# Attention on one NeuronCore: the 64-row first query block and key chunk handled as 128 rows

## The chip, the cores and the metric

The kernel runs on one core of a Trainium2 chip. The metric is the device time of one execution in microseconds (us), the median over several runs. The engines of the core are PE (TensorE, with its weight loads listed apart as PEld), DVE (VectorE), ACT (ScalarE), POOL (GpSimd) and SP (SyncE, which issues the DMAs here).

## The reference

Inputs are `q`, `k`, `v` of shape 4 x 8 x 576 x 64 and a gate `f` of shape 4 x 8 x 576. For each batch entry and head:

```python
cum = cumsum(log(clip(f, 1e-4, 1)))
scores = q @ k.T / 8 + (cum[i] - cum[j])      # -1e9 where j > i
attn = softmax(scores)                         # with 1e-9 added to the sum
x = attn @ v
```

The heads are put side by side (2304 rows of 512) and go through two dense layers: first `max(x@w1, x@w2, x@w3) @ w_out` with 768 hidden columns, then `g(x @ w_in) @ w_out` with 2048 hidden columns, where `g` is a quotient of polynomials.

## The kernel before

The sequence of 576 rows is cut into five query blocks that are also the five key chunks: rows 0 to 64 and then four times 128 rows (`Q0`, `Q1`, L20 and L21). Blocks 0, 1, 2 form group 0 (320 queries), blocks 3 and 4 form group 1 (256 queries). Two heads of a batch entry form a `Pair`; a `Unit` is one head of a pair in one group. Batch entry 0 is done as four pairs with group 0 alone and then four pairs with group 1 alone; the other three entries as twelve pairs with both groups. That makes 20 pairs and 64 units, 32 of each group.

What a pair does ahead of its units (`prepare`, L301): `load` and `load_v` bring natural rows of q, k and v into tiles `qn`, `kn`, `v` of 128 partitions x 5 chunks x 2 heads x 64, by `load_nat` (L221). Block 0 has one DMA of its own, 64 partitions, both heads (L223); the others share a DMA for each head. `transposed` (L283) turns the blocks on PE into one PSUM tile `tk` or `tq`, one transposition for each block (L288). For block 0 it takes 64 rows of the tile and a 64 x 64 corner of the identity. A pair turns its keys of group 0 even if it has queries of group 1 alone, so there are 36 transpositions of a 64-row block: 20 of k and 16 of q. ACT, DVE and POOL then make the operands of the score product from the PSUM tile.

What a unit does, in three steps of the main loop (L537): in its first step `scores` (L321) multiplies query block `i` by all keys up to its end. The first six pairs use one product in full float32 (L340), the others two products in the split format (L342, L343). The query block is the stationary operand, 64 columns wide for block 0, the keys are streamed. DVE masks the scores, negates them and takes the row minimum (L344), ACT takes the exponential with the row sum (L350). `normalise` (L352) makes reciprocals on DVE and scales `e` on POOL (L360). `begin` sets, for group 0, the 64 unused rows of the row sums to one with a small POOL memset (L319). In the next step `turn` (L362) transposes the blocks of `e` on PE into a PSUM tile `tp`, key chunk by key chunk (L381), and ACT copies a bank of them to `pt` (L385). Key chunk 0 gives 64 partitions there, and block 0, which has chunk 0 alone, is transposed from 64 rows. `pt` is allocated for each pair and group under a tag with one buffer (L367). In the step after that `attend` (L387) multiplies, for both heads, `v` of each key chunk (stationary, 64 columns, head 0 to PSUM partitions 0 to 63, head 1 to the others) by the transposed probabilities, in float32 (L399). For key chunk 0 both operands have 64 partitions. There are 32 calls of `attend` that do work.

Around this, `fill` (L502) inserts work of other stages a fixed number of times in each step: conversions of weights for the first dense layer and later for the second (L151 to L170: DMA, ACT, DVE, POOL), and products of the first dense layer (L429 to L431, L453 to L455). After the last unit the rest of the first layer and the conversion of `w_in` follow, then the second layer (L669 to L720), to the end. In the first four pairs every fresh PSUM tile is first written by two products of a constant tile (`exercised`, L77). The instructions of each engine are put in order by the tile framework, which schedules with its own simulated timeline (`schedule_with_timeline_sim=True`), but for some DMAs that are kept in program order and the second layer, whose order is written out. In most of the calls of `attend` the scheduler runs the two passes of head 0 on key chunk 0 ahead, by themselves, and the rest later in one run.

Of the kernel before, what the change touches and what calls it, by code (L numbers as in the profile page):

```python
# [18 lines left out]

Q0 = [0, 64, 192, 320, 448]  # L20
Q1 = [64, 192, 320, 448, 576]  # L21
GQ = [(0, 320), (320, 576)]
GBLK = [(0, 1, 2), (3, 4)]

# [10 lines left out]
def kernel(  # L35
# [100 lines left out]
    for qf in qfs:  # L136
        nc.vector.tensor_copy(qf[D : D + 2], ones[0:2, :NA])


    w1t, wot = {}, {}  # L140

# [78 lines left out]

    def load_nat(dst, src, b, h0, i0, i1):  # L221
        if i0 == 0:
            nc.sync.dma_start(dst[0:D, 0], src[b, h0 : h0 + 2, 0:D].rearrange("h p d -> p h d"))  # L223
            i0 = 1
        for h in range(2):
            nc.sync.dma_start(
                dst[:, i0:i1, h], src[b, h0 + h, Q0[i0] : Q1[i1 - 1]].rearrange("(c p) d -> p c d", p=P)
            )
# [3 lines left out]
    class Pair:  # L232
# [50 lines left out]
        def transposed(self, nat, g, which):  # L283
            lo, hi = GQ[g]
            t = exercised(ps_t.tile([P, 512], F32, name=f"t{which}_{self.n}_{g}", tag="t"), self.n)
            for i in GBLK[g]:
                nr = Q1[i] - Q0[i]
                nc.tensor.transpose(  # L288
                    t[:, Q0[i] - lo : Q1[i] - lo],
                    nat[0:nr, i].rearrange("p h d -> p (h d)"),  # L290
                    ident[0:nr, 0:nr],
                )
            return t[:, : hi - lo]

        def copies(self):
# [12 lines left out]
    class Unit:  # L308
# [6 lines left out]
        def begin(self):  # L315
            self.st = apool.tile([P, 9], F32, name=f"st_{self.nm}", tag="st", bufs=3)
            self.rs = apool.tile([P, 2, 3], F32, name=f"rs_{self.nm}", tag="rs", bufs=3)
            if self.g == 0:
                nc.gpsimd.memset(self.rs[D:P, 0, 0:1], 1.0)  # L319

        def scores(self, i):  # L321
            p, h, g = self.pair, self.h, self.g
            if not p.whole:
                (k1, k2), (q1, q2) = k_split(p.ik[h]), q_split(g, p.iq[g][h])
            nr = Q1[i] - Q0[i]
            qs = slice(Q0[i] - GQ[g][0], Q1[i] - GQ[g][0])
            keys = Q1[i]
            self.e[i] = apool.tile([P, keys], F32, name=f"e{i}_{self.nm}", tag=f"e{i}_{h}")
            e = self.e[i]
            st = self.st  # L330
            n0 = 3 * (i - GBLK[self.g][0])
            nm = st[:nr, n0 : n0 + 2]
            l = self.rs[:nr, 0, i - GBLK[self.g][0] : i - GBLK[self.g][0] + 1]
            parts = [(0, keys)] if keys <= 512 else [(0, 320), (320, keys)]
            off = S - keys if nr == P else S - P - Q0[i]
            for n, (a, z) in enumerate(parts):
                sp = exercised(ps_s.tile([P, 512], F32, name=f"s{i}_{n}_{self.nm}", tag="s"), p.n)
                if p.whole:
                    kf, qf = kfs[p.ik[h]][: D + 2], qfs[p.iqf[h]][: D + 2]
                    nc.tensor.matmul(sp[:nr, : z - a], qf[:, qs], kf[:, a:z], start=True, stop=True)  # L340
                else:
                    nc.tensor.matmul(sp[:nr, : z - a], q1[:, qs], k1[:, a:z], start=True, stop=False)  # L342
                    nc.tensor.matmul(sp[:nr, : z - a], q2[:, qs], k2[:, a:z], start=False, stop=True)  # L343
                nc.vector.tensor_tensor_reduce(  # L344
                    out=e[:nr, a:z], in0=sp[:nr, : z - a], in1=mask[:nr, off + a : off + z],
                    scale=-1.0, scalar=3.0e38 if n == 0 else nm[:, 0:1],
                    op0=ALU.add, op1=ALU.min, accum_out=nm[:, n : n + 1],
                )
            m = nm[:, len(parts) - 1 : len(parts)]
            nc.scalar.activation(e[:nr], e[:nr], AF.Exp, bias=m, scale=-1.0, accum_out=l)  # L350

        def normalise(self):  # L352
            blks = GBLK[self.g]
            n = len(blks)
            nc.vector.tensor_scalar_add(self.rs[:, 0, :n], self.rs[:, 0, :n], 1.0e-9)
            nc.vector.reciprocal(self.rs[:, 1, :n], self.rs[:, 0, :n])  # L356
            for j, i in enumerate(blks):
                nr = Q1[i] - Q0[i]
                e = self.e[i]
                nc.gpsimd.tensor_scalar(e[:nr], e[:nr], self.rs[:nr, 1, j : j + 1], 0.0, op0=ALU.mult, op1=ALU.add)  # L360

        def turn(self, bank):  # L362

            g, p = self.g, self.pair
            hi = GQ[g][1]
            if g not in p.pt:
                p.pt[g] = apool.tile([P, 2, GCOLS[g]], F32, name=f"pt_{self.nm}", tag=f"pt{g}")  # L367
            pt = p.pt[g][:, self.h]
            chunks = GBANK[g][bank]
            tp = exercised(ps_t.tile([P, 512], F32, name=f"tp{bank}_{self.nm}", tag="t"), self.pair.n)  # L370
            base = GCH[g][chunks[0]][0]
            n = 0
            for c in chunks:
                col, q0 = GCH[g][c]
                kr = Q1[c] - Q0[c]
                for i in GBLK[g]:
                    if i < c:
                        continue
                    nr = Q1[i] - Q0[i]
                    dst = col - base + Q0[i] - q0  # L380
                    nc.tensor.transpose(  # L381
                        tp[:kr, dst : dst + nr], self.e[i][:nr, Q0[c] : Q1[c]], ident[:nr, :nr]
                    )
                n += hi - q0
            nc.scalar.activation(pt[:kr, base : base + n], tp[:kr, :n], AF.Copy)  # L385

        def attend(self):  # L387

            p, h, g = self.pair, self.h, self.g
            if h == 0:  # L390
                return
            lo, hi = GQ[g]
            w = hi - lo
            ot = exercised(ps_o.tile([P, 512], F32, name=f"o_{self.nm}", tag="o"), p.n)
            order = list(GCH[g].items())
            for j, (c, (col, q0)) in enumerate(order):
                kr = Q1[c] - Q0[c]
                for i in range(2):
                    nc.tensor.matmul(  # L399
                        ot[SIDES[i][0], q0 - lo : w], p.v[:kr, c, i], p.pt[g][:kr, i, col : col + hi - q0],  # L400
                        start=(j == 0), stop=(j == len(order) - 1),
                    )
            x = mpool.tile([P, 2, w], F32R, name=f"x_{self.nm}", tag=f"x{g}", bufs=(6, 8)[g])
            nc.scalar.activation(x[:, 0], ot[:, :w], AF.Copy)
            nc.vector.tensor_tensor(x[:, 1], ot[:, :w], r32(x[:, 0]), op=ALU.subtract)
            xt[p.b, p.hp, g] = x
# [389 lines left out]
```

## Time and profile before

| | us |
|---|---|
| median of 3 runs | 1014.16 (1014.15 to 1014.49) |
| the profiled execution | 1014.65 |
| its span, from the first instruction to the last | 1012.8 |
| PE busy | 984.6 (97%) |
| DVE busy | 750.6 (74%) |
| ACT busy | 613.5 (61%) |
| POOL busy | 286.7 (28%) |

Busy time of PE is counted with the modelled ends of the products, which overlap: one that starts 0.11 us after another is shown with 0.27 us. What a product costs in a run of products is the distance from its start to the next start. Attention with the first dense layer in its gaps takes the first 520 us or so, the rest of the first layer with the conversion of `w_in` until about 607 us, the second layer the rest.

### The profile page before, as it was taken

What the parts mean: (1) busy time and instruction counts of PE and PEld (TensorE: products, weight loads), DVE (VectorE), ACT (ScalarE), POOL (GpSimd) and SP (SyncE); (2) the same over time, 40 slices, a digit from 0 to 9 for tenths busy, and PEclk for the clock granted to TensorE, in tenths of its full rate; (3) what the DMA queues carried; (4) which work ended last, traced back from release to release, by engine and by line L of the source; (5) the groups of instructions that cost most, each with busy time, mean ns of one, the idle gap of its engine ahead of it and who ended that gap; (6) DMA issues with size and microseconds to landing.
All of it is one profiled execution on the core that took longest, in us unless ns stands there. A gap on an engine that the chain in (4) does not pass through costs nothing.

```text
span 1012.8 us, 16900 instructions
## 1 busy us (share of the span) xinstructions
PE 984.6 (97%) x5780; PEld 831.2 (82%) x5780; DVE 750.6 (74%) x1744; ACT 613.5 (61%) x1409; POOL 286.7 (28%) x498
## 2 busy tenths in 40 slices
PE   8989999999999999999998989999999999999998
PEld 5657778887888888988898987888888888899997
DVE  4779984555677676644349676988988888899997
ACT  4775665656655566554434336766766666677775
POOL 1545763543554554443326440000000000000000
PEclk9998999999999999999999999999999999999999
DMA  4574223213444355221034529301001100200000
GB/s 122 162 213 132 79 57 89 47 41 104 119 128 151 104 154 179 81 59 48 1 116 146 177 80 344 128 1 49 35 1 63 42 1 1 95 10 1 32 1 32
DMA packets 118453, 86.69 MB, mean 86 GB/s; under 512 B 67280, under 2 KB 103136, under 8 KB 118368
## 3 DMA queue, kind: packets, MB, share of 16 engines
q1 hardware_dynamic: 118368, 85.62, 27.9%
q8 instruction: 46, 0.75, 0.3%
q14 instruction: 39, 0.32, 0.1%
HBM read 62.90 MB, written 22.69 MB: 85 GB/s over the span
## 4 chain that ended last, share of the span: by engine, by line
PE 77%; DVE 14%; issue 3%; DMA 3%; ACT 2%; POOL 1%; SPq 0%; DVEq 0%; POOLq 0%; ACTq 0%
PE oo L719 7%; PE oo L720 7%; PE oo L718 6%; PE o L399 6%; PE hq L669 6%; PE hq L671 6%; PE hq L670 6%; PE tp L381 5%; PE h L429 5%; PE h L430 4%; PE h L431 4%; PE s L342 2%; PE x2p L453 2%; PE x2p L455 2%; PE x2p L454 2%
## 5 line engine op out<-in xcount | busy, mean ns | idle before, releaser
L429 PE MATMUL h<-x,w1h 128*128 128x320 f32 (+1 forms) x576 | 176.9, 307 | 2.1 <-DVE m L436 2.0
L430 PE MATMUL h<-x,w1h 128*128 128x320 f32 (+1 forms) x576 | 173.0, 300 | 0.0
L431 PE MATMUL h<-x,w1l 128*128 128x320 f32 (+1 forms) x576 | 172.7, 300 | 0.0
L360 POOL TENSOR_SCALAR e<-e,rs 64x64 f32<-64x64 f32 (+4 forms) x160 | 88.6, 565 | 114.5 <-DVE rs L356 87.9
L350 ACT ACTIVATE e<-e,st 64x64 f32<-64x64 f32 (+4 forms) x160 | 89.3, 558 | 51.7 <-DVE st L344 48.9
L429 PEld LDWEIGHTS h<-x,w1h 128*128 128x128 f32 x576 | 110.3, 192 | 8.8 <-DVE m L436 3.7
L719 PE MATMUL oo<-wp,gh 128*128 128x512 f32 x288 | 112.8, 392 | 0.0
L718 PE MATMUL oo<-wp,gh 128*128 128x512 f32 x288 | 112.4, 390 | 0.0
L430 PEld LDWEIGHTS h<-x,w1h 128*128 128x128 f32 x576 | 110.2, 191 | 2.2 <-issue 2.0
L344 DVE CUSTOM_DVE_ANT_0 e<-s,mask 128x320 f32<-128x320 f32 (+3 forms) x160 | 68.1, 432 | 57.6 <-PE s L343 37.3
L431 PEld LDWEIGHTS h<-x,w1l 128*128 128x128 f32 x576 | 110.0, 191 | 0.1
L720 PE MATMUL oo<-wp,gl 128*128 128x512 f32 x288 | 108.8, 392 | 0.0
L678 ACT ACTIVATE s<-hq 128x512 f32<-128x512 f32 (+1 forms) x80 | 44.3, 554 | 97.2 <-PE hq L671 97.1
L385 ACT ACTIVATE pt<-tp 128x384 f32<-128x384 f32 (+3 forms) x160 | 69.8, 471 | 31.6 <-PE tp L381 28.7
L399 PE MATMUL o<-pt,v 128*64 128x256 f32 (+3 forms) x512 | 83.0, 371 | 0.3 <-ACT pt L385 0.3
L381 PE MATMUL tp<-ident,e 128*128 128x128 f32 (+2 forms) x480 | 81.4, 278 | 0.6 <-POOL e L360 0.5
L681 DVE SCALAR_TENSOR_TENSOR s<-s,ab,u 128x512 f32<-128x512 f32 (+1 forms) x80 | 55.8, 698 | 31.8 <-ACT u L679 31.6
L671 PE MATMUL hq<-x,wil 128*128 128x512 f32 (+1 forms) x192 | 70.4, 366 | 0.0
L669 PE MATMUL hq<-x,wih 128*128 128x512 f32 (+1 forms) x192 | 70.4, 366 | 0.0
L670 PE MATMUL hq<-x,wih 128*128 128x512 f32 (+1 forms) x192 | 70.3, 366 | 0.0
L453 PE MATMUL x2p<-hh,wo 128*128 128x320 f32 (+1 forms) x192 | 59.6, 314 | 7.2 <-POOL hh L440 5.9
L381 PEld LDWEIGHTS tp<-ident,e 128*128 128x128 f32 (+2 forms) x480 | 54.3, 132 | 13.6 <-issue 7.0
(128 smaller groups left out, 2444.6 us busy)
## 6 DMA issues: line engine op xcount, KB each, us to landing
raw_w<-in_moe_w_dram SPq DMA_DIRECT2D x18, 512.0 KB
raw_wp<-in_moe_w_out_dram SPq DMA_DIRECT2D x32, 256.0 KB
wpd<-wp SPq DMA_DIRECT2D x32, 256.0 KB
raw_wi<-in_moe_w_in_dram SPq DMA_DIRECT2D x32, 256.0 KB
wp<-wpd SPq DMA_DIRECT2D x10, 768.0 KB
x2d<-xo SPq DMA_DIRECT2D x16, 320.0 KB
out_dram<-ob SPq DMA_DIRECT2D x18, 256.0 KB
kn<-in_k_dram SPq DMA_DIRECT2D x32, 128.0 KB
```

The source lines that it names most:

```text
L350: nc.scalar.activation(e[:nr], e[:nr], AF.Exp, bias=m, scale=-1.0, accum_out=l)
L381: nc.tensor.transpose(tp[:kr, dst : dst + nr], self.e[i][:nr, Q0[c] : Q1[c]], ident[:nr, :nr])
L399: nc.tensor.matmul(ot[SIDES[i][0], q0 - lo : w], p.v[:kr, c, i], p.pt[g][:kr, i, col : col + hi - q0], start=(j == 0), stop=(j == len(orde ...
L429: nc.tensor.matmul(hp_[:, :w], wh[:, j, dc], xs[dc][:, 1], start=(dc == NDC - 1), stop=False)
L430: nc.tensor.matmul(hp_[:, :w], wh[:, j, dc], xs[dc][:, 0], start=False, stop=False)
L431: nc.tensor.matmul(hp_[:, :w], wl[:, j, dc], xs[dc][:, 0], start=False, stop=(dc == 0))
L669: nc.tensor.matmul(hp_[:, :w], wih[:, dc, fs], xh, start=(dc == 0), stop=False)
L670: nc.tensor.matmul(hp_[:, :w], wih[:, dc, fs], xl, start=False, stop=False)
L671: nc.tensor.matmul(hp_[:, :w], wil[:, dc, fs], xh, start=False, stop=(dc == NDC - 1))
L718: nc.tensor.matmul(o, g[0][:, ts_], wh_, start=(fc == 0), stop=False)
L719: nc.tensor.matmul(o, g[0][:, ts_], wl_, start=False, stop=False)
L720: nc.tensor.matmul(o, g[1][:, ts_], wh_, start=False, stop=(fc == NF2 - 1))
```

## The change

Block 0 and key chunk 0 are given 128 rows. The loads of block 0 bring rows 0 to 127 of q, k and v. The transpositions of block 0 take 128 rows and the whole identity, and write 128 columns, of which the upper 64 are then overwritten by block 1. The scores of block 0 are computed for 128 queries against 64 keys. The attention product on chunk 0 reads 128 rows of `v` and of `pt`. Since the transposition of chunk 0 still gives only 64 rows, two lasting tiles `pts` take the place of the tile for each pair, and the lower half (partitions 64 to 127) of the columns of chunk 0 is set to zero once at the start. The memset of the unused row sums goes.

```diff
+    pts = []
+    for g in range(2):
+        pts.append(apool.tile([P, 2, GCOLS[g]], F32, name=f"pt{g}", tag=f"pt{g}"))
+        col = GCH[g][0][0]
+        nc.gpsimd.memset(pts[g][D:P, :, col : col + GQ[g][1] - GQ[g][0]], 0.0)
...
     def load_nat(dst, src, b, h0, i0, i1):
         if i0 == 0:
-            nc.sync.dma_start(dst[0:D, 0], src[b, h0 : h0 + 2, 0:D].rearrange("h p d -> p h d"))
+            nc.sync.dma_start(dst[:, 0], src[b, h0 : h0 + 2, 0:P].rearrange("h p d -> p h d"))
             i0 = 1
...
             for i in GBLK[g]:
-                nr = Q1[i] - Q0[i]
-                nc.tensor.transpose(
-                    t[:, Q0[i] - lo : Q1[i] - lo],
-                    nat[0:nr, i].rearrange("p h d -> p (h d)"),
-                    ident[0:nr, 0:nr],
-                )
+                at = Q0[i] - lo
+                nc.tensor.transpose(t[:, at : at + P], nat[:, i].rearrange("p h d -> p (h d)"), ident)
             return t[:, : hi - lo]
...
-            if self.g == 0:
-                nc.gpsimd.memset(self.rs[D:P, 0, 0:1], 1.0)
...
-            nr = Q1[i] - Q0[i]
-            qs = slice(Q0[i] - GQ[g][0], Q1[i] - GQ[g][0])
+            nr = P
+            qs = slice(Q0[i] - GQ[g][0], Q0[i] - GQ[g][0] + P)
...
-            off = S - keys if nr == P else S - P - Q0[i]
+            off = S - P - Q0[i]
...
-                nr = Q1[i] - Q0[i]
                 e = self.e[i]
-                nc.gpsimd.tensor_scalar(e[:nr], e[:nr], self.rs[:nr, 1, j : j + 1], 0.0, op0=ALU.mult, op1=ALU.add)
+                nc.gpsimd.tensor_scalar(e, e, self.rs[:, 1, j : j + 1], 0.0, op0=ALU.mult, op1=ALU.add)
...
             if g not in p.pt:
-                p.pt[g] = apool.tile([P, 2, GCOLS[g]], F32, name=f"pt_{self.nm}", tag=f"pt{g}")
+                p.pt[g] = pts[g]
...
-                    nr = Q1[i] - Q0[i]
                     dst = col - base + Q0[i] - q0
-                    nc.tensor.transpose(
-                        tp[:kr, dst : dst + nr], self.e[i][:nr, Q0[c] : Q1[c]], ident[:nr, :nr]
-                    )
+                    nc.tensor.transpose(tp[:kr, dst : dst + P], self.e[i][:, Q0[c] : Q1[c]], ident)
...
             for j, (c, (col, q0)) in enumerate(order):
-                kr = Q1[c] - Q0[c]
                 for i in range(2):
                     nc.tensor.matmul(
-                        ot[SIDES[i][0], q0 - lo : w], p.v[:kr, c, i], p.pt[g][:kr, i, col : col + hi - q0],
+                        ot[SIDES[i][0], q0 - lo : w], p.v[:, c, i], p.pt[g][:, i, col : col + hi - q0],
                         start=(j == 0), stop=(j == len(order) - 1),
                     )
```

## Rows read from the trace of the kernel before

**Rows 1.** The page: span, and busy time with its share and instructions by engine.

```profile
span 1012.8 us, 16900 instructions
```

**Rows 2.** Busy time by stretch: PE, PEld, DVE, ACT, POOL, granted clock, DMA share, GB/s.

```profile
10.00:65.00 55.00, 54.42 (x264) 34.73 (x265) 33.10 (x107) 39.01 (x109) 20.48 (x36) 1.00 0.61 169
65.00:150.00 85.00, 75.48 (x458) 61.21 (x457) 79.04 (x184) 52.67 (x129) 56.27 (x70) 0.95 0.39 108
150.00:310.00 160.00, 158.56 (x1125) 133.69 (x1124) 96.12 (x325) 97.69 (x277) 75.65 (x156) 0.98 0.31 86
380.00:520.00 140.00, 139.96 (x1011) 121.16 (x1010) 67.41 (x231) 69.98 (x198) 54.63 (x105) 1.00 0.24 73
```

**Rows 3.** Chain of waits by line, in 10 to 65, 65 to 150, 150 to 310, 310 to 380.

```profile
by line: PE s L340 20.7%; PE s L81 20.5%; PE tp L81 14.6%; PE o L399 13.0%; PE tp L381 12.5%; PE tk L288 5.6%; PE tq L288 3.2%; PE o L81 2.9%; DMA kf<-ncd 2.6%; PE tq L81 2.1%; PE tk L81 1.7%; issue 1.0%; DVE st L344 0.2%; DVE e L344 0.1%
by line: DVE cv_w L163 11.9%; issue 11.8%; DVE cv_w L166 6.6%; DVE cv_wo L163 6.6%; DVE cv_w L162 6.5%; DVE e L344 6.1%; DVE m L436 5.3%; DVE cv_wo L161 5.1%; DVE cv_wo L166 4.4%; DVE cv_wo L162 4.0%; DVE cv_w L161 3.8%; DVE k2s L266 2.9%; 
by line: PE o L399 17.5%; PE tp L381 13.8%; PE h L429 12.7%; PE h L430 12.3%; PE h L431 12.0%; PE s L342 6.3%; PE s L343 5.8%; PE x2p L454 3.1%; PE tq L288 3.1%; PE x2p L453 3.0%; PE x2p L455 2.9%; PE tk L288 2.9%; issue 1.2%; DVE q1s L278 
by line: DMA raw_wp<-in_moe_w_out_dram 11.4%; PE o L399 7.6%; issue 7.0%; PE h L429 6.7%; PE h L431 6.1%; PE h L430 6.1%; DVE cv_wp L163 4.1%; PE tp L381 4.0%; PE x2p L453 3.6%; DVE q1s L278 3.4%; DMA wpd<-wp 3.0%; DVE cv_wp L161 2.8%; PE x
```

**Rows 4.** PE's timeline, transpositions without 64-row blocks: start us, us, line, form (rows*columns), count.

```profile
154.56 0.71 PE L381 MATMUL tp<-ident,e 128*128 128x128 f32 x5
155.03 0.39 PE L342 MATMUL s<-k1s,q1s 128*128 128x320 f32 x1
```

**Rows 5.** PE's timeline around the transposition of k of one pair.

```profile
190.93 0.27 PE L381 MATMUL tp<-ident,e 128*64 128x128 f32 x1
191.13 0.64 PE L288 MATMUL tk<-ident,kn 64*128 64x64 f32 x3
191.53 0.36 PE L342 MATMUL s<-k1s,q1s 128*128 128x256 f32 x1
```

**Rows 6.** PE's timeline, six transpositions of one unit with block 0 among them.

```profile
160.58 1.00 PE L381 MATMUL tp<-ident,e 128*128 128x128 f32 x6
161.34 0.45 PE L342 MATMUL s<-k1s,q1s 128*128 128x448 f32 x1
```

**Rows 7.** PE's timeline in the run of `attend` that begins at 157.71, in narrow stretches.

```profile
157.71 0.43 PE L399 MATMUL o<-pt,v 64*64 64x256 f32 x1
158.29 0.44 PE L399 MATMUL o<-pt,v 128*64 128x256 f32 x2
158.77 0.39 PE L399 MATMUL o<-pt,v 128*64 128x256 f32 x2
159.20 0.39 PE L399 MATMUL o<-pt,v 128*64 128x256 f32 x2
```

**Rows 8.** Weight loads of the split score products: busy us, mean ns of one, idle before.

```profile
L342 PEld LDWEIGHTS s<-k1s,q1s 128*128 128x128 f32 x132 | 25.1, 191 | 5.9 <-issue 2.3 <-DVE st L344 1.3 <-POOL k1s L267 1.1
L342 PEld LDWEIGHTS s<-k1s,q1s 128*64 128x64 f32 x24 | 3.3, 138 | 1.9 <-POOL q2s L281 1.1 <-POOL k1s L267 0.4 <-DVE cv_wp L162 0.4
```

**Rows 9.** Block 0 of `e`: 10 to 65 (380 to 520 alike), 150 to 310, 310 to 380.

```profile
L381 PE MATMUL tp<-ident,e 64*64 64x64 f32 x8 | 1.9, 243 | 0.0
L381 PE MATMUL tp<-ident,e 64*64 64x64 f32 x12 | 2.9, 243 | 0.0
L381 PE MATMUL tp<-ident,e 64*64 64x64 f32 x4 | 1.0, 243 | 0.0
```

**Rows 10.** Groups by form that differ in rows, 128 and 64: ACT, then PE.

```profile
L350 ACT ACTIVATION_READ_ACCUMULATOR e<-e,st 128x1 f32 x128 | 24.0, 188 | 0.0
L350 ACT ACTIVATION_READ_ACCUMULATOR e<-e,st 64x1 f32 x32 | 6.0, 188 | 0.0
L399 PE MATMUL o<-pt,v 128*64 128x256 f32 x256 | 35.3, 392 | 0.0
L399 PE MATMUL o<-pt,v 64*64 64x256 f32 x64 | 19.9, 402 | 0.3 <-ACT pt L385 0.3
```

**Rows 11.** POOL's timeline up to the first scaling of `e`.

```profile
0.88 0.58 POOL L86 MEMSET mask<- 128x576 f32 x1
1.52 0.09 POOL L319 MEMSET rs<- 64x1 f32 x1
...
15.45 1.22 POOL L360 TENSOR_SCALAR e<-e,rs 64x64 f32<-64x64 f32 x3 [12.85 <-DVE rs L356]
```

**Rows 12.** SP's timeline: the load of block 0 of the k transposed at 191.13.

```profile
171.52 0.60 SPq L223 DMA_DIRECT2D kn<-in_k_dram  x1
```

## The prediction

> **What bounds the kernel now.** I read the page first, for the span [rows 1], then the busy time by stretch, which cuts the run where the work changes [rows 2]. The reader is to see that PE is busy for nearly all of 10 to 65, 150 to 310 and 380 to 520 us, and that between 65 and 150 it is DVE that has no room (79.04 of 85 us). The chain of waits says the same and is the stronger evidence, since busy time of PE counts overlapping ends: in 10 to 65 the PE lines listed hold 96.8% of the chain, in 150 to 310 they hold 95.4%, in 65 to 150 it is the conversions of weights on DVE, and in 310 to 380 the longest item is the load of `raw_wp` [rows 3]. So a microsecond taken off PE is worth a microsecond in three stretches, and little in the two others. After 520 us nothing of the change remains.
>
> Then I read PE's timeline start by start, since a product in a run costs the distance to the next start. Five transpositions without a 64-row block begin at 154.56 and the score product behind them at 155.03: 0.11 us each and 0.03 for the last [rows 4]. Around a 64-row block it is different. From the transposition before the k tile (190.93) to the 64-row one (191.13) are 0.20 us, and from 190.93 to the product behind the three of k (191.53) are 0.60 [rows 5]; four starts at the pace of rows 4 would take 3 x 0.11 + 0.03 = 0.36. PE pauses where a product's row count changes between 128 and 64, on the way in and on the way out.
>
> **The change part by part.**
> *Transpositions of q and k.* 36 blocks of 64 rows become 128 rows. Each now costs 0.60 where 0.36 would do [rows 4, 5], so 0.24 us goes for each, 36 x 0.24 = 8.6. The extra 64 columns streamed are in the 0.11, which is the price of a 128-row block.
> *Transposition of block 0 of `e`.* Six transpositions with it take 160.58 to 161.34, 0.76 us [rows 6]; at the pace of rows 4, 5 x 0.11 + 0.03 = 0.58. That is 0.18 for each of 32 [rows 9]: 5.8.
> *Attention product on chunk 0.* In a run of `attend` a pass on 256 columns starts 0.43 / 2 = 0.215 us after the one before (158.77 to 159.20 is two passes). Chunk 0 has two passes for 158.29 - 157.71 = 0.58, and the two after it take 0.48 [rows 7]. Without the step from 64 to 128 rows the first two would take 0.48 (the first after the entry is the longer one, as it is at 158.29) and the next two 0.43: 1.06 becomes 0.91, 0.15 for each of 32: 4.8. A 64-row pass is no cheaper than a 128-row one (402 against 392 ns in the groups, [rows 10]), so the added rows cost nothing. The pauses on entering and leaving the 64-column product stay.
> *Scores of block 0.* 24 units have a pair of split products; its weight loads grow from 64 to 128 columns, 138 to 191 ns, 0.053 each [rows 8]. The first load of a pair mostly runs under the product before it, the second can't hide under a product of 64 columns: between 0.053 and 0.106 for each unit, I take 0.07, a loss of 1.7. The eight units in full float32 (L340) no longer stand at 64 columns; no row here prices that. Bounds are 2 x 0.053 lost and two pauses of 0.09 (0.20 - 0.11, [rows 5]) won; I take 0.08 won, near the middle of the upper part, 0.6.
> *DVE, ACT, POOL on 128 rows.* The ACT read of the accumulator takes 188 ns on 64 and on 128 rows [rows 10]; the streamed lengths don't change. Nothing, and these engines have room in the stretches that count [rows 2]; were it not so, some 10 ns for each of 32 units on each engine.
> *Memsets.* On POOL 32 of 0.09 us go; two come, of 640 and 512 columns, by the 0.58 for 576 columns about 0.65 and 0.5 [rows 11]. The one on `pt0` waits until the buffer is free of `nch`, that is until its store has landed, near 10 us. What stands behind it in POOL's queue is the scaling of `e` at 15.45, after 12.85 us of idle POOL [rows 11]. That cover gone, it would be some 1 us, once.
> *Lasting `pt`.* The tag had one buffer before, and `attend` of a pair comes two units ahead of the next write in the same columns. No new wait; PE would be late first if there were one, since its transpositions would stand behind ACT's copy.
> *Loads.* 56 DMAs of block 0 move 64 KB and not 32 KB, the same number of issues on SP, so no queue is passed. The load for the k transposed at 191.13 was issued at 171.52 [rows 5, 12], 19 us ahead. With the DMA engines busy 24 to 61% in the three stretches [rows 2], that hides it; without the cover, 32 KB at the 169 GB/s of the first stretch would be 0.2 us a load, 11 us in all and the upper bound of a loss.
>
> **The sum by stretch.** A unit of group 0 carries one block of `e`, on average one of q or k: 0.18 + 0.24 = 0.42, with its `attend` 0.57. Units by stretch are 8, 12, 4, 8 [rows 9]. In 10 to 65: 8 x 0.42, four calls of `attend` 0.6, L340 0.6: 4.6. In 150 to 310: 12 x 0.57 less 11 x 0.07: 6.1. In 380 to 520: 8 x 0.57 less 0.56: 4.0. Together 14.7. In 310 to 380 there are 2.0 and in 65 to 150 about 1.5 (four k blocks, four `attend`), counted at nothing because DMA and DVE hold those ends. Of the 14.7 I take 0.93, a little under the PE share of the chain: 13.7. From the profiled execution, 1014.65, that gives 1000.95; it stands 0.49 above the median of the runs, 1014.16, so the forecast is 1000.5.
>
> A statement that speaks against the change is weighed here by itself. Rows 10 show a 64-row pass as long as a 128-row one. The Trainium skill, TensorEngine Tiling (Array Packing), section Theoretical Speedup, has products of at most 64 rows up to twice as fast, if tiles are packed. By it the change would give up half of 128 passes of about 0.21 us, some 14 us, and the sum would be near nothing. That hangs on two 64-row products side by side in different rows of the array; here all lie on partitions 0 to 63. It is the fourth rival.
>
> **The rivals.**
> *All of it counts.* If the stretches with DVE and DMA at their end also shorten, because PE's products stand between the conversions there, the full 18.2 us go: 996.0. For it: PE is busy 75 of 85 us even from 65 to 150. Against: the chain there. Chance 0.14.
> *Freed PE time turns into waits.* A unit goes PE, DVE, ACT, DVE, POOL, PE, ACT, PE. If PE then waits on this round instead of pausing, half of 14.7 is kept: 1006.8, down to a third, 1009. For it: the order is the scheduler's and can shift anywhere, and DVE is the next engine in line. Against: the dense products lie ready as filling. Chance 0.20.
> *It does not reach the end of the waits.* The change does what it says and the bound is elsewhere after all: 1012.5 to 1014.2. Against it rows 3. Chance 0.05.
> *64 rows are the cheap ones.* Two 64-row passes run at once somewhere and lose that: 0.5 x 0.215 x 128 = 13.8 against 13.7 won, 1014.3. Against it rows 10. Chance 0.03.
> *Slower: the pauses belong to what stays.* If PE pauses because of the 64-column products next to these (chunk 0 still turns into 64 partitions, `attend` is still 64 columns wide), no pause goes, and PE carries in its bound stretches what is added: 24 x 2 x 0.053 = 2.5 of weight loads and, on 68 transpositions, 64 more columns at 0.055 (half of 0.11), 3.7. That makes 1020.4; it decides once fewer than a third of the pauses go (6.2 of 18.2). Against it: the k tile has 128 columns throughout and pauses all the same [rows 5]. Chance 0.05.
>
> **How the numbers follow.** The forecast keeps 0.53. About 0.2%, 2 us, is what a measurement of this kernel tells from no change. Faster: forecast, all of it, waits, 0.53 + 0.14 + 0.20 = 0.87. Same: no reach and cheap 64 rows, 0.08. Slower 0.05. The range leaves out the 0.13 of the last three and some 0.05 at its rims: from 995.5 (all 18.2 and the loads of the scores under cover) to 1009.0 (a third of 14.7).
>
> **What would show it.** Right: runs of transpositions at 0.11 us throughout, three of k in 0.49 from first start to last end and not 0.64; no pause between chunk 0 and chunk 1 in `attend`; the pairs of score products of block 0 some 0.05 to 0.1 longer; the stretch up to the last `attend` shorter by 13 to 14, and that after it unchanged. Wrong: pauses that remain at the same places (the last rival); starts that stay apart with a wait on ACT, POOL or DVE where the pause was (the second); a lower granted clock in 65 to 150, now 0.95 [rows 2], since PE would be idle more; a late first scaling of `e`, or a wait of L288 on its load.

## The result and the profile after

The changed kernel takes 997.54 us (median of 4 runs, 994.15 to 997.93), the one before 1014.33 beside it (median of 4, 1014.15 to 1015.82): ratio 0.9826, interval 0.981 to 0.9843. That is 16.8 us by the medians where 13.7 were forecast, and inside the range of 995.5 to 1009.0. The profiled execution took 997.18 us.

The page of the changed kernel: span, busy time by engine, and the chain of waits by engine.

```profile
span 995.4 us, 16863 instructions
...
PE 966.3 (97%) x5780; PEld 837.3 (84%) x5780; DVE 749.4 (75%) x1744; ACT 611.2 (61%) x1409; POOL 284.8 (29%) x468
...
PE 81%; DVE 12%; issue 2%; DMA 2%; POOL 1%; ACT 1%; SPq 0%; DVEq 0%; POOLq 0%; ACTq 0%
```

The number of PE's products is the same, 5780, and PE's busy time is 966.3 us where it was 984.6, in a span that is 17.4 us shorter [rows 1]: the pauses had stood in the busy time, since the modelled ends of the products overlap. The other engines' busy times fell by 1.2 to 2.3 us, so the added rows cost them nothing that shows. POOL has 30 instructions less: 32 memsets went and two came.

Busy time by stretch, the columns of rows 2:

```profile
10.00:65.00 55.00, 54.14 (x290) 39.55 (x289) 37.88 (x120) 43.50 (x121) 22.61 (x35) 1.00 0.74 201
65.00:150.00 85.00, 75.56 (x479) 65.01 (x480) 77.08 (x182) 50.67 (x128) 54.33 (x70) 0.94 0.38 107
150.00:310.00 160.00, 158.30 (x1172) 140.46 (x1171) 101.41 (x341) 102.36 (x291) 78.52 (x148) 1.00 0.36 100
380.00:520.00 140.00, 140.00 (x1025) 127.50 (x1024) 70.59 (x224) 65.78 (x184) 53.45 (x97) 1.00 0.25 74
```

Read the counts, not PE's busy time: the same 55, 85, 160 and 140 us now hold 290, 479, 1172 and 1025 products where 264, 458, 1125 and 1011 stood [rows 2].

PE's timeline shows where they gained. First three transpositions of `e` and the three of k behind them, then a run of `attend` between other work, then six transpositions with block 0 among them that don't follow `attend`:

```profile
157.53 0.49 PE L382 MATMUL tp<-ident,e 128*128 128x128 f32 x3
157.86 0.49 PE L297 MATMUL tk<-ident,kn 128*128 128x128 f32 x3
158.10 0.37 PE L345 MATMUL s<-k1s,q1s 128*128 128x256 f32 x1
...
151.77 2.16 PE L397 MATMUL o<-pt,v 128*64 128x256 f32 x18
153.86 0.87 PE L382 MATMUL tp<-ident,e 128*128 128x128 f32 x6
...
176.63 0.82 PE L382 MATMUL tp<-ident,e 128*128 128x128 f32 x6
177.21 0.36 PE L427 MATMUL h<-x,w1h 128*128 128x256 f32 x1
```

The three of k take 0.49 us from first start to last end, as forecast, and 0.24 to the next start; before it was 0.64 and 0.40 [rows 5]. Six transpositions with block 0 take 0.58 to the next start and not 0.76 [rows 6]. The run of `attend` on 18 products takes 2.09 us (153.86 - 151.77); before it was 2.24, here with the product that follows it:

```profile
157.71 2.31 PE L399 MATMUL o<-pt,v 64*64 64x256 f32 x18
159.95 0.36 PE L342 MATMUL s<-k1s,q1s 128*128 128x192 f32 x1
```

That is 0.15, the forecast for each call. So the pauses went at every place that was named. The stretches don't add up as forecast, though. The scalings of block 0 of `e` on POOL mark the same work in both kernels. Here are the first (for the changed kernel alone; that of before is in rows 11), 8th, 9th, 20th and 32nd, before and then after:

```profile
57.55 0.71 POOL L360 TENSOR_SCALAR e<-e,rs 64x64 f32<-64x64 f32 x2 [2.39 <-DVE rs L356]
157.45 0.31 POOL L360 TENSOR_SCALAR e<-e,rs 64x64 f32<-64x64 f32 x1 [4.96 <-DVE rs L356]
293.57 0.31 POOL L360 TENSOR_SCALAR e<-e,rs 64x64 f32<-64x64 f32 x1 [1.05 <-DVE rs L356]
494.94 0.31 POOL L360 TENSOR_SCALAR e<-e,rs 64x64 f32<-64x64 f32 x1 [4.03 <-DVE rs L356]
```

```profile
15.58 0.72 POOL L362 TENSOR_SCALAR e<-e,rs 128x64 f32<-128x64 f32 x2 [5.15 <-DVE rs L359]
52.63 0.71 POOL L362 TENSOR_SCALAR e<-e,rs 128x64 f32<-128x64 f32 x2 [2.04 <-PE o L397]
149.73 0.32 POOL L362 TENSOR_SCALAR e<-e,rs 128x64 f32<-128x64 f32 x1 [2.63 <-DVE rs L359]
280.86 0.82 POOL L362 TENSOR_SCALAR e<-e,rs 128x64 f32<-128x64 f32 x2 [1.20 <-DVE rs L359]
479.65 0.71 POOL L362 TENSOR_SCALAR e<-e,rs 128x64 f32<-128x64 f32 x2 [3.69 <-DVE rs L359]
```

The distances shrank by 5.1 us up to the 8th, 2.8 to the 9th, 5.0 to the 20th and 2.6 to the 32nd. The last product of `attend` starts at 519.0 before and 505.5 after, the second layer at 607.5 and 591.7; with the ends of the spans that makes -1.8, +2.3 and +1.6. By the last `attend` it is 13.6, as forecast. The other 3.9 came behind it. Of these the 1.6 of the second layer, whose code is untouched, lies within the 0.8 to 1.7 that nearly every run below shows against the same execution of before, so most of it is that execution's own; where the 2.3 come from was not taken apart.

Two more readings are used below. **PE's account** splits the distances between starts of PE's products, up to the end of the first layer. *Around `attend`* are those with a product into its PSUM tile `o` on either side (with the constant tile's products that write `o` first), each up to 0.5 us. *Other products* are the rest, each up to the usual distance of the same two forms in these runs (plus 0.04). What is over is called *waits*. Which distance is usual is a choice: with others, the fall of the other products from before to after comes out between 14.4 and 17.9 us, where the table has 15.9. A *piece* is an unbroken run of products of `attend`. **The clock**: from run to run the time falls by 0.4 to 0.6 us for each 0.001 of mean granted clock (slopes over 23, 19 and 9 runs of before; those of the other kernels, over 4 to 12 runs, scatter from 0.95 to none), so that comparisons of one or two us are read with the mean clock beside them. What is put down to the clock in this way is argued and not shown.

| us | other products | around `attend` | waits | pieces of `attend` |
|---|---|---|---|---|
| before | 470.6 | 95.4 | 37.7 | 64 |
| after | 454.7 | 93.3 | 38.7 | 68 |
| q and k alone | 462.0 | 99.2 | 33.5 | 68 |
| scores alone | 470.4 | 99.9 | 33.4 | 67 |
| scores and turn | 463.6 | 99.9 | 33.1 | 68 |
| `attend` alone | 469.2 | 92.1 | 41.9 | 67 |
| after without `attend` | 454.5 | 97.4 | 37.6 | 67 |
| loads alone | 470.8 | 99.8 | 37.9 | 70 |
| before, head 1 first | 473.9 | 73.5 | 42.1 | 38 |
| after, head 1 first | 458.7 | 67.5 | 42.5 | 37 |

### The profile page after: what moved, and what is told of

Its sections match the earlier page's. It is cut to its first block, busy times and chain, and to the rows that moved or that the text cites. A ratio compares the mean times of both kernels' runs of the same rounds, so it can differ in the third digit from the quotient of the medians.

```text
span 995.4 us, 16863 instructions
## 1 busy us (share of the span) xinstructions
PE 966.3 (97%) x5780; PEld 837.3 (84%) x5780; DVE 749.4 (75%) x1744; ACT 611.2 (61%) x1409; POOL 284.8 (29%) x468
## 4 chain that ended last, share of the span: by engine, by line
PE 81%; DVE 12%; issue 2%; DMA 2%; POOL 1%; ACT 1%; SPq 0%; DVEq 0%; POOLq 0%; ACTq 0%
PE hq L667 7%; PE hq L669 7%; PE hq L668 7%; PE oo L717 7%; PE oo L718 7%; PE oo L716 7%; PE o L397 6%; PE h L427 5%; PE h L428 5%; PE h L429 5%; PE tp L382 4%; PE x2p L451 2%; PE s L345 2%; PE x2p L453 2%; PE x2p L452 2%
## 5 line engine op out<-in xcount | busy, mean ns | idle before, releaser
L353 ACT ACTIVATE e<-e,st 128x64 f32<-128x64 f32 (+4 forms) x160 | 89.3, 559 | 57.2 <-DVE st L347 53.1
L362 POOL TENSOR_SCALAR e<-e,rs 128x64 f32<-128x64 f32 (+4 forms) x160 | 89.0, 571 | 85.4 <-DVE rs L359 62.0
L347 DVE CUSTOM_DVE_ANT_0 e<-s,mask 128x320 f32<-128x320 f32 (+3 forms) x160 | 68.4, 433 | 58.1 <-PE s L346 41.9
L397 PE MATMUL o<-pt,v 128*64 128x256 f32 (+2 forms) x512 | 80.2, 369 | 0.0
L382 PE MATMUL tp<-ident,e 128*128 128x128 f32 (+1 forms) x480 | 77.0, 278 | 2.0 <-POOL e L362 1.3
L718 PEld LDWEIGHTS oo<-wp,gl 128*128 128x128 f32 x288 | 54.0, 188 | 11.7
```

The lines of the kernel that those rows point to most:

```text
L382: nc.tensor.transpose(tp[:kr, dst : dst + P], self.e[i][:, Q0[c] : Q1[c]], ident)
L397: nc.tensor.matmul(ot[SIDES[i][0], q0 - lo : w], p.v[:, c, i], p.pt[g][:, i, col : col + hi - q0], start=(j == 0), stop=(j == len(order) - 1),
L718: nc.tensor.matmul(o, g[1][:, ts_], wh_, start=False, stop=(fc == NF2 - 1))
```

## The experiments

Each kernel was timed beside the kernel before on the same chip; ratios are against that.

**The parts one by one.** The transpositions of q and k, with their loads:

```diff
+            n0 = D if src is v else P
+            nc.sync.dma_start(dst[0:n0, 0], src[b, h0 : h0 + 2, 0:n0].rearrange("h p d -> p h d"))
...
+                at = Q0[i] - lo
+                nc.tensor.transpose(t[:, at : at + P], nat[:, i].rearrange("p h d -> p (h d)"), ident)
```

> The kernel before with the transpositions of q and k alone on 128 rows (and the loads of q and k that this needs; v, the scores, the probabilities and attend stay on 64). Theory, that each 64-row product costs PE a pause and that PE bounds most of attention: 36 blocks at 0.24 us are 8.7 us, 6.5 of them in the stretches that PE bounds, so 1014.3 less 6.5 to 8.7, 1005.6 to 1007.8. The trace shows three transpositions of k in 0.49 us and not in 0.64. Rival, that the gain comes from the order the scheduler happened to find: the parts don't add up to the whole, and this one alone may land anywhere from 1008 to 1018.

Measured: 1006.13 us, ratio 0.9908 (0.9891 to 0.9924), 9.3 less. The other products fell by 8.6, the forecast of this term. Around `attend` stand 3.8 more, in four more pieces, and the waits are 4.2 less: these two cancel, and the time agrees with the term in part because they do. The mean clock was 0.990 against 0.987 of before, by the slopes some 1.0 to 1.4 of the 9.3.

The scores of block 0 alone, whose added half is used by nothing, and then the scores with the scaling and the transposition of `e`:

```diff
-            if self.g == 0:
-                nc.gpsimd.memset(self.rs[D:P, 0, 0:1], 1.0)
...
+            nr = P
+            qs = slice(Q0[i] - GQ[g][0], Q0[i] - GQ[g][0] + P)
...
+            off = S - P - Q0[i]
```

> The kernel before with the score products of block 0 alone widened to 128 queries; the transpositions take the upper 64 rows as before, so the added half is computed and not used. The small memset of the row sums goes. Theory: 24 pairs of weight loads at 0.07 are 1.7 lost, against 0.6 won by the full float32 products, 1 us slower, 1015.3; the trace has the start to start distance of the two products and of the one behind them at 0.11 and not 0.06. Rival, that the load hides under its neighbours: 1013.7. Rival of order: a change of several us either way.

Measured: 1013.47 us, ratio 0.9978 (0.9969 to 0.9987), 2.2 less and not 1 more. The other products stayed (470.6, 470.4). What was mis-sized is the entry into the products in full float32. Here it stands before and after, the product of the constant tile and then the score products:

```profile
19.20 0.40 PE L81 MATMUL s<-warm 128*128 128x512 f32 x1
19.53 0.27 PE L340 MATMUL s<-kf,qf 66*64 66x64 f32 x1
```

```profile
17.68 0.39 PE L84 MATMUL s<-warm 128*128 128x512 f32 x1
17.91 0.33 PE L343 MATMUL s<-kf,qf 66*128 66x64 f32 x2
18.08 0.50 PE L382 MATMUL tp<-ident,e 128*128 128x128 f32 x3
```

From 0.33 to 0.23 us on the way in; the distance between two passes fell from 0.107 to 0.058, the step out of them from 0.15 to 0.11: 0.19 in all for each unit, 1.5 won for eight. The split pairs lost 0.053 each (second product to the next start, 0.057 before and 0.110), 24 x 0.053 = 1.3. Won and lost cancel on PE. By the slopes the clock gives 1.3 to 1.9 of the 2.2 (0.9905 against 0.987), but among the twelve runs of this kernel itself the slope is 0.08, so where the 2.2 come from stays open.

```diff
+                nc.gpsimd.tensor_scalar(e, e, self.rs[:, 1, j : j + 1], 0.0, op0=ALU.mult, op1=ALU.add)
...
+                    nc.tensor.transpose(tp[:kr, dst : dst + P], self.e[i][:, Q0[c] : Q1[c]], ident)
```

> The kernel before with block 0 of the scores and of the probabilities on 128 rows, transposed from 128 rows; the loads, the transpositions of q and k and attend stay on 64. Theory: 32 x 0.18 won by the transpositions is 5.8, 0.6 won by the full float32 scores and 1.7 lost by the wider weight loads of the split scores, 4.7 in all, about 4 in the stretches that PE bounds: 1009.6 to 1010.3. Rival of order: anywhere from 1008 to 1018. Rival that the weight loads cost twice as much: 1012.

Measured: 1006.5 us, ratio 0.9915 (0.9897 to 0.9934), 8.6 less. Against the scores alone the other products fell by 6.8, 0.21 for each of 32 blocks and not 0.18. The steps in the trace of before give 0.185 on the mean, 5.9 in all: a 64-row block starts 0.094 later than a 128-row one would (0.203 for 0.109), the next product 0.064 later (0.173), and the one after that 0.026 later if the product behind the pause has 64 columns, as in rows 6, or 0.055 if it has 128. Where the other 0.9 went is not known.

The product of `attend` on 128 rows, with the lasting `pt` and the load of v; and the lasting `pt` by itself:

```diff
+    pts = []
+    for g in range(2):
+        pts.append(apool.tile([P, 2, GCOLS[g]], F32, name=f"pt{g}", tag=f"pt{g}"))
+        col = GCH[g][0][0]
+        nc.gpsimd.memset(pts[g][D:P, :, col : col + GQ[g][1] - GQ[g][0]], 0.0)
...
+                p.pt[g] = pts[g]
...
+                        ot[SIDES[i][0], q0 - lo : w], p.v[:, c, i], p.pt[g][:, i, col : col + hi - q0],
```

> The kernel before with attend alone on 128 rows of key chunk 0: the lasting zeroed tiles, v loaded with 128 rows, the products on 128 rows; q, k, scores and the transpositions stay on 64. Theory: 32 runs of attend are each 0.15 shorter (10 products in 1.33 and not 1.48 us, 18 in 2.09 and not 2.24), 4.8 in all and some 4 in the stretches that PE bounds: 1009.5 to 1010.3. Rival, that the lasting tiles and not the row count give the gain: the same time, but the runs of attend stay at 1.48 and 2.24. Rival of order: anywhere from 1008 to 1018.

> The kernel before with the lasting pt tiles alone, not zeroed, and attend on 64 rows of key chunk 0 as before. Asked is why attend alone on 128 rows made its runs shorter by the forecast 0.15 us and the kernel by only 0.6. Theory, that the time went into waits of the stretch from 65 to 150 which DVE bounds, by another order, and that the lasting tile is neutral: within 2 us of before. Rival, that a lasting tile makes writes wait for readers where a fresh one did not: 3 to 5 us slower than before, with waits of ACT on PE at pt.

Measured: 1014.66 us, ratio 0.9994 (0.9978 to 1.0009), for the first, 1014.62 and 1.0004 (0.9992 to 1.0017) for the second. The lasting `pt` costs nothing that can be measured. The runs of `attend` did shorten. PE's timeline of the first: a run of 18 products and what follows it, and a piece of head 0 on chunk 0 that the scheduler sends ahead by itself:

```profile
159.70 2.16 PE L405 MATMUL o<-pt,v 128*64 128x256 f32 x18
161.78 0.42 PE L349 MATMUL s<-k1s,q1s 128*128 128x320 f32 x1
...
167.16 0.75 PE L405 MATMUL o<-pt,v 128*64 128x320 f32 x2
167.84 0.47 PE L350 MATMUL s<-k2s,q2s 66*128 66x448 f32 x1
```

The run takes 2.08 us, again some 0.15 under the 2.24 of before. The piece takes 0.68 us for two passes and has pauses on both of its sides, as before: it is 64 columns wide among products of 128, which the change leaves. In PE's account the part around `attend` fell by 3.3 us, where 4.7 would be all 32 calls, with three more pieces; the waits rose by 4.2. The clock was 0.986 against 0.987, by the slopes 0.6 to 0.9 against this kernel.

The same question from the other side, the whole change without its part in `attend`:

```diff
-                p.pt[g] = pts[g]
+                p.pt[g] = apool.tile([P, 2, GCOLS[g]], F32, name=f"pt_{self.nm}", tag=f"pt{g}")
...
+                kr = Q1[c] - Q0[c]
...
-                        ot[SIDES[i][0], q0 - lo : w], p.v[:, c, i], p.pt[g][:, i, col : col + hi - q0],
+                        ot[SIDES[i][0], q0 - lo : w], p.v[:kr, c, i], p.pt[g][:kr, i, col : col + hi - q0],
```

> The changed kernel with attend taken back: pt allocated for each pair, chunk 0 of attend on 64 rows, v loaded with 64 rows; the rest on 128. Theory of additive parts, with attend worth what its pauses are: 4 us slower than the changed kernel, 12 to 14 faster than before. Rival, that attend is worth as little here as alone: the same as the changed kernel within 1.5 us, 16 to 18 faster than before.

Measured: 998.46 us, ratio 0.984 (0.9823 to 0.9857), so `attend` is worth 1.4 us in the whole, give or take 2.4. The rival stands nearer than the theory: PE gains the time here, and the kernel gets little of it.

**The loads alone.**

```diff
-            nc.sync.dma_start(dst[0:D, 0], src[b, h0 : h0 + 2, 0:D].rearrange("h p d -> p h d"))
+            nc.sync.dma_start(dst[:, 0], src[b, h0 : h0 + 2, 0:P].rearrange("h p d -> p h d"))
```

> The kernel before with the loads of block 0 alone at 128 rows (q, k and v); the upper half is loaded and not used. Theory: they land far ahead, within 2 us of before. Rival, the cover is gone because the attention runs just in time: up to 11 us slower, with waits of PE on kn, qn or v. Rival, that their issue on SP, 0.37 us in the trace of after and 0.60 before, frees SP's queue and other loads come sooner: 1 to 3 us faster.

Measured: 1019.68 us, ratio 1.0053 (1.0035 to 1.0071): 5.4 more, at a mean clock no lower (0.989 against 0.988). No change was expected, so this missed. PE's account tells the place and not a transfer: other products 470.8 and waits 37.9 are those of before, but around `attend` stand 99.8 us and not 95.4, in 70 pieces and not 64. The order that the scheduler wrote had changed, with 4.4 us for six more pieces. Two more pauses each would be some 1.2; the next experiment shows what the rest is.

**The order.** If pieces of `attend` cost that much, the ones that before already has should too. A piece can go ahead because head 0, ready a step earlier, stands first in the sum. With head 1 first, nothing of `attend` is ready before the rest:

```diff
-                for i in range(2):
+                for i in (1, 0):
```

On before, and on the changed kernel:

> The kernel before with head 1 first in attend and nothing else. Theory, that the early pieces of attend cost PE two pauses each wherever rows stand: attend in some 37 runs and not 64, 27 us less of PE around attend as in the changed kernel, and 10 to 15 us off the time, 1000 to 1005. Rival, that this was worth so much only after the change freed PE: under 5 us.

> The changed kernel with the two heads in attend taken in the other order, head 1 first. In the trace the two passes of head 0 on chunk 0 run ahead alone, 32 times, 0.58 us for 256 and 0.68 for 320 queries, with a pause on entering and leaving the 64-column products. With head 1 first nothing of attend is ready before its last part, so it runs in one piece and head 0's passes run beside head 1's. Theory, that pauses at a change of the product's shape are paid on PE wherever they stand: 32 x 0.6 is 19 us less on PE, and where PE bounds 8 to 16 us of it shows: 982 to 990. Rival, that the early passes fill time in which PE would wait: the same as the changed kernel within 2 us. Rival, that the output of attend comes later and the dense layer waits for it: slower by 2 to 5.

Measured: 999.07 us, ratio 0.9847 (0.983 to 0.9863), on before, 15.5 less; and 981.62 us, ratio 0.9685 (0.9666 to 0.9704), on the changed kernel, 14.3 less than that kernel by the ratios. The second beats both kernels. PE's timeline of each, one call of `attend` whole, with its 20 products between its neighbours; first on before, then on the changed kernel:

```profile
158.94 2.31 PE L399 MATMUL o<-pt,v 64*64 64x256 f32 x20
161.18 0.41 PE L342 MATMUL s<-k1s,q1s 128*128 128x320 f32 x1
```

```profile
177.05 0.28 PE L429 MATMUL h<-x,w1l 128*128 128x256 f32 x1
177.17 0.28 PE L427 MATMUL h<-x,w1h 128*128 128x256 f32 x1
177.38 2.17 PE L397 MATMUL o<-pt,v 128*64 128x256 f32 x20
179.47 0.88 PE L382 MATMUL tp<-ident,e 128*128 128x128 f32 x6
```

All 20 products take 2.24 us on before and 2.09 on the changed kernel, as long as 18 took while the other two stood elsewhere for 0.68 or 0.57. So two passes that cost over half a us by themselves cost nothing in the run, which is more than two pauses. The reason is in rows 7: the `x2` there are two products that start together, 0.007 us apart in the trace, and such a pair takes 0.215, no longer than a single pass of 256 columns. The two passes of a lone piece follow each other, so the two of a pair belong to the two heads, which write different halves of the PSUM partitions. A piece of head 0 that goes ahead has no partner: of its 0.57, 0.43 are the two passes themselves (0.53 of the 0.68 with 320 queries), the rest is the pause on the way out, and 0.09 more go on the way in. By this estimate two thirds of what a piece costs are lost pairing and one third pauses. The theory, which put all of it on pauses, named the smaller part. In the account 95.4 became 73.5 and 93.3 became 67.5, in 38 and 37 pieces; about 4 of these 22 and 26 us came back as waits and 3 to 4 in the other products.

With the order made steadier in this way, three parts were asked again. The loads on before with head 1 first (the edit of the loads above):

> The kernel before with head 1 first in attend and the loads of block 0 at 128 rows. The loads alone made the kernel before 5.4 us slower, and the time around attend in its trace was 4.4 us longer, in 70 runs and not 64. Theory, that the loads cost nothing and that the scheduler cut attend into more pieces: with head 1 first it can't, so the same as the kernel before with head 1 first within 1.5 us. Rival, that the loads themselves cost: 4 to 6 us slower than that kernel.

Measured: 1000.81 us, ratio 0.9861 (0.9845 to 0.9878), 1.4 above the same without them by the ratios, 1.7 by the medians, at a clock of 0.9865 against 0.988 (0.6 to 0.9 by the slopes). The interval of the 1.4 is 2.3 either way, and both kernels have 38 pieces. So most of the 5.4 was the order, and these runs can't tell the cost of the transfers themselves from nothing.

`attend` on 64 rows again, and the transpositions of q and k on 64 rows again, each taken out of the changed kernel with head 1 first (the edits above, the other way round):

> The changed kernel with head 1 first in attend, and attend taken back to 64 rows of chunk 0 with pt for each pair. Alone and in the whole, attend on 128 rows was worth 0.6 and about 1.5 us where its runs were 4.8 us shorter. Theory, that more pieces of attend or another order ate the rest: with attend in one piece either way the 32 x 0.15 show, 4 to 5 us slower than the changed kernel with head 1 first, 27 to 28 faster than before. Rival, that PE waits there and the shorter runs are worth nothing: within 1.5 us of it, 31 to 32 faster than before.

> The changed kernel with head 1 first in attend, and the transpositions of q and k taken back to 64 rows, with their loads. Theory of additive pauses: 36 x 0.24 is 8.7, of which 6.5 to 8.7 show, 23 to 25 us faster than before. Rival, that the 9 us this part gave alone were in part the order: 27 us or more faster than before.

Measured: 984.5 us, ratio 0.9707 (0.9693 to 0.9721), and 988.04 us, ratio 0.9746 (0.9728 to 0.9764). By the ratios `attend` is worth 2.2 there (give or take 2.4), q and k 6.2 (2.6): 29.7 and 25.8 us faster than before, each between its theory and its rival. In PE's account the first has 72.0 around `attend` and not 67.5, the second 468.2 of other products and not 458.7: 4.5 and 9.5, where 4.8 and 8.6 were forecast. What PE loses the time shows at a half and at two thirds, and the second ran at a clock of 0.985 against 0.987. So neither pair is settled, and where the other half of `attend` goes stays open.

## Why the prediction was right, and where it was not

**The mechanism held.** PE pauses where its products change between 64 and 128 rows, and the pauses went at every place named. The sum over PE is close, in part by luck: without waits its account fell by 18.0 us, where the steps gave 18.2, but with 15.9 for 13.3 in the other products and 2.1 for 4.8 around `attend`. The time fell by 16.8 by the medians, more than the 14.7 of the three stretches, of which 0.93 were to show.

**q and k: right.** 8.6 forecast, 8.6 in the account of that part alone, 9.3 in its time, a little of that the clock.

**The block of `e`: mis-sized.** 5.8 - 1.7 + 0.6 = 4.7 were forecast for `e` and its scores, 8.6 came in the time of that part alone. The account gives 7.0: 6.8 for the transpositions (0.21 each and not 0.18), 1.5 won in full float32, all of the upper bound of two pauses (8 x 0.18 = 1.4), where 0.6 was taken, and 1.3 lost on the split pairs and not 1.7. Of the 1.6 over 7.0 the clock would give 0.5 to 0.7 by the slopes (0.9885 against 0.987); the interval of the time, 6.7 to 10.5 us, holds the rest, which was not taken apart.

**`attend`: right per call, wrong in the time.** The 0.15 for each run is there, but the time shows 0.6 alone, 1.4 in the whole and 2.2 with the order steadier, and not 4.5. The step that failed is that PE's time in these stretches is the kernel's, term by term. In the whole change part of it went into four more pieces (68 against 64): 2.1 around `attend` and not 4.8. With the order steadier PE has the gain, 4.5, and the time still shows half of it; why stays open.

**Nothing for the loads: right for the transfers only.** They stay hidden as far as the runs can tell; but the step looked at engines and queues and left out that the order of PE's instructions is made anew for every edit. By itself the edit costs 5.4 us, most of it through the order. All the kernels above with the order of heads as it was, but that with the lasting `pt` alone, have 67 to 70 pieces where before has 64, so the order is a term of some us in every one of these comparisons, the whole change among them.

**The stretches: only the sum was right.** 65 to 150 us was counted at nothing and gave 2.8, more than the 1.5 that stand there. The chain does not explain it: PE has 5.8% of it there before and 25.2% after, all lines added up, and the granted clock stayed, 0.94 for 0.95, so the cause is open. 310 to 380 was put at nothing because of the load of `raw_wp`, the longest single item; but the PE lines shown there hold 34.1% together [rows 3], so a part of its 2.0 should have counted. 10 to 65 gave 5.1 for 4.3, while from 150 to the last `attend` 5.8 came where 9.4 were due. Behind it, where nothing was to change, 3.9 came. Part of this is where the clock fell. Both profiled executions have about as much time at the lower level after 10 us (20.4 and 20.5 us), but at other places. Before, then after, in 6 us slices (columns of rows 2):

```profile
240.00:246.00 6.00, 4.82 (x27) 2.73 (x25) 3.98 (x14) 4.96 (x15) 3.55 (x9) 1.00 0.70 186
246.00:252.00 6.00, 5.74 (x30) 5.77 (x31) 5.33 (x20) 3.61 (x11) 2.22 (x5) 0.72 0.23 52
```

```profile
360.00:366.00 6.00, 4.23 (x34) 3.76 (x32) 5.64 (x16) 3.67 (x11) 3.27 (x7) 1.00 0.39 101
366.00:372.00 6.00, 5.94 (x32) 5.34 (x33) 3.33 (x18) 2.95 (x11) 2.24 (x3) 0.72 0.59 177
```

Each has one slice at a granted clock of 0.72 behind one in which PE waited: 0.28 x 6 / 0.5 = 3.4 us at 1.2 GHz, up to 1.7 us of work lost, before in the third stretch and after in the one up to the 32nd unit. So the gain of 5.0 may be that much too high and the 2.6 that much too low.

**The memsets and the lasting `pt`: right.** POOL's timeline of the changed kernel has the two where they were put, 0.52 and 0.63 us, the second until 10.4 us, and the first scaling of `e` starts at 15.58 where it was 15.45 [rows 11]:

```profile
1.52 0.52 POOL L146 MEMSET pt<- 64x512 f32 x1
9.80 0.63 POOL L146 MEMSET pt<- 64x640 f32 x1 [7.06 <-DMA ncd<-nch]
```

**The rivals.** That all of it counts (996.0) fits the result better than the forecast does: the interval of the ratio is 15.9 to 19.3 us, which holds this rival's 18.2 and not the 13.7. Freed time that turns into waits is seen with `attend` alone (41.9 for 37.7) and with head 1 first (42.1 and 42.5), and not in the whole change (38.7). That the pauses belong to what stays is refuted by three transpositions of k in 0.49 us, and that 64 rows are the cheap ones by the runs of `attend` with 128 rows, which are the shorter. The Trainium skill, TensorEngine Tiling (Array Packing), Key Properties, has it that a change of tiling mode drains TensorE. The pauses of about 0.1 us on each side agree with that; the page gives no price. No run here has two 64-row products side by side in different rows of the array, so its Theoretical Speedup was not put to the test for rows. On the same rows, for the two halves of the PSUM partitions, they do run side by side: with head 1 first on before, all 64-row passes of the two heads start in pairs, 0.007 us apart.

## What to carry to other kernels

Keep PE's consecutive products in one shape: where rows don't set a product's time, padding 64 to 128 with zeros or unused rows removes a pause on each side, and what that is worth is counted from the distances between starts, pause by pause. Look for lone pieces of an accumulation that a scheduler sends ahead because their operands are ready: putting the operand that comes last first kept the run whole and was worth nearly as much as the whole padding, 14.3 to 15.5 us for 16.8. A lone piece costs most where its products would have run beside others that are not yet ready. Where a scheduler makes the order anew for every edit, count its pieces before a difference of a few us is put down to the edit.

## What the runs showed that was not expected

The wider load is the quicker to issue. SP's part of the load of block 0 of k (shortest, median, longest ns; first and last start in us), before and after:

```profile
L223 SPq DMA_DIRECT2D kn<-in_k_dram x20: 601/602/1085, 1.2 to 439.5; - x20
```

```profile
L232 SPq DMA_DIRECT2D kn<-in_k_dram x20: 367/368/562, 1.2 to 425.1; - x20
```

64 partitions take 0.60 us and 128 take 0.37, for twice the bytes. The loads alone give the same 0.37, so it is the shape of the load and no other part of the change.

A product with 64 columns is not always a break. In the changed kernel a transposition with a 64-column stationary starts 0.11 us after one with 128 columns, and the next one with 128 columns 0.11 after it (medians of 71 and of 12 steps), with no pause; the split scores of before with 64 columns were left after 0.06. The products in full float32 with 64 columns, those of `attend` and of the first six pairs, are entered with a pause of about 0.1: 177.17 to 177.38 above is 0.21 where the two products before it start 0.12 apart. The runs tell the forms apart, not why.
